# A second written order for a fused delta-rule attention and cosine feed-forward kernel

## The chip, the cores and the metric

The kernel runs on one core of a Trainium2 chip. The metric is device time in microseconds (us) of one execution. The core has five engines that run beside each other, each strictly in its own program order: TensorE (PE in the profile; its weight loads are PEld), VectorE (DVE), ScalarE (ACT), GpSimd (POOL) and SyncE (SP), which here only issues DMAs. Where one engine needs what another makes, it waits on a semaphore.

## The reference

There are two stages, in float32. The first is a gated delta rule, per batch and head, over 768 steps with a 48 x 48 state:

```python
k_n = k / (np.linalg.norm(k, axis=-1, keepdims=True) + 1e-06)
for t in range(S):
    y[:, :, t] = np.einsum('bhd,bhde->bhe', q[:, :, t], state)
    v_old = np.einsum('bhde,bhd->bhe', state, kt)
    state = state + bt[:, :, :, None] * np.einsum('bhd,bhe->bhde', kt, vt - v_old)
...
h = x @ w_in
g = h * np.cos(h)
return (g @ w_out).astype(np.float32)
```

Shapes: q, k, v are (4, 8, 768, 48), beta (4, 8, 768). The outputs of the 8 heads side by side are the 3072 x 384 input `x` of the second stage; `w_in` is 384 x 2048 and `w_out` 2048 x 384.

## The kernel before

**Attention.** The 768 steps are cut into 24 units of 32. For unit n, TensorE transposes keys and queries (`turn`, later units by DMA blocks and a VectorE transpose), multiplies them with each other (`gram`), and VectorE scales and masks the products (`gram_keys`, `gram_queries`). A unit needs the inverse of a unit triangular 32 x 32 matrix per head. For units 0 to 3 that is done by elimination on half blocks: `rows` (TensorE, L701) spreads rows, `eliminate` (L721, L728) subtracts them, on VectorE for units 0 and 1 (groups r = 0 and 1, four steps each) and on GpSimd for units 2 and 3 together (r = 2, eight steps, each fed by a copy on ScalarE, `rows_copy`). `fold`, `fold_in`, `fold_off` and `unfold` bring the blocks in and out. From unit 4 on, pairs m of units are inverted on GpSimd (`inv`, L791 and L798), with a round trip through DRAM before (`gram_put`, `gram_get`) and after (`put`, `get`). Then come `state` (products with the state), `right` (L843), `solve` (for the first units `solve_half`, `half_out`, `between`, `between_out` and `solve`), `solve_out` (L901), `update` and `update_out` (the new state), `within`, `within_out`, `features` and `features_out` (the transposed x). The step from one unit's state to the next is serial.

**Weights.** 28 pieces of the weights come in as 64-bit words and are made float32 by a chain per piece t: `weights` (DMA), `split` (ScalarE), `shift` (VectorE, two instructions, L497 and L502) and `add` (GpSimd, L506).

**Feed-forward.** Tokens go in 12 groups p of 256. For p = 0 and 1 the hidden layer is plain (`hidden`, L974), from p = 2 on it is a fast-multiplication scheme of 20 smaller products (`layer`, L1152) over sums of inputs (`x_sum`, L1067) and of weights (`in_sums`, L1114). The gate h cos h is four tasks: `turns` (ScalarE), `rest` (VectorE), `cos` (ScalarE), `gate` (VectorE, L1034). The output layer is plain for p = 0 (`out`, L1175) and a seven-product Strassen scheme after it (`out`, L1232), with sums `left` (L1248) and `right` with two indices (L1261), and results added up by `collect` (L1284).

**The order.** The program is a list of 2143 tasks, each with its emit function, its dependences and the buffers that it makes and uses. `Order.run` emits them in the order of `Order.LINE`, a written list of task numbers (the place of the task in the order in which it was added), and every engine's instructions are pinned in that order. No planner runs: an engine whose next task is not ready waits, with all that stands behind it. `Order.OTHER` is a set of tasks that run on their second engine: `fold` and `unfold` on ScalarE and not VectorE, `weigh`, `left`, `in_sums` and `right` on GpSimd and not VectorE, `x_sum` on VectorE and not GpSimd. Some buffers are scarce: the PSUM tag `h` has three banks, which `rows`, `hidden`, `layer` and the last group's products share; tag `two` has one, through which each of `turn`, `gram`, `solve` and `update` passes in turn.

## Time and profile before

| | |
|---|---|
| runs | 653.87, 645.26, 649.0 us, median 649.0 |
| the profiled execution | 647.59 us, its span 645.8 us |
| mean granted TensorE clock | 0.987 |
| busy | PE 616.5 us, PEld 577.8, DVE 509.5, POOL 450.7, ACT 266.4 |
| instructions | 28227, of which PE 12306 matmuls and as many weight loads |
| instruction queue q8 | 96 packets, 1.57 MB |

The page gives busy time and instructions of each engine, then the span in 40 slices of 16 us with the busy share in tenths and the granted clock of TensorE (PEclk), then the DMA queues, the chain that ended last, and groups of instructions with the idle time ahead of them and what ended it. The page's 40 slices average the clock; asked by its own edges, the trace grants half speed (0.50) from 32.03 to 38.86, from 45.69 to 52.51 and from 73.00 to 76.40 us, and full speed elsewhere as far as it records.

### The profile page before, as it was taken

How to read it: one execution, taken by the hardware profiler on the slowest of the kernel's cores; microseconds unless marked ns; L12 is line 12 of the kernel's file. 1: busy time of each engine (PE TensorE's matmuls, PEld its weight loads, DVE VectorE, ACT ScalarE, POOL GpSimd, SP SyncE). 2: the span in 40 equal slices, each digit the busy share in tenths (PEclk: the TensorE clock that was granted, in tenths of full speed). 3: DMA queues.
4: the chain of work that ended last, by engine and by line, in shares of the span. 5: the costliest groups of instructions: out<-in, count | busy, mean ns of one | idle time of the engine just before them, and what ended most of it. 6: DMA issues, size and time to landing. Idle time of an engine off the chain costs nothing.

```text
span 645.8 us, 28227 instructions
## 1 busy us (share of the span) xinstructions
PE 616.5 (95%) x12306; PEld 577.8 (89%) x12306; DVE 509.5 (79%) x948; ACT 266.4 (41%) x469; POOL 450.7 (70%) x788
## 2 busy tenths in 40 slices
PE   5869899999999999999999999999999999999997
PEld 4758788886989999999899999999999999999997
DVE  7788788889899988888788878766877668667681
ACT  3645556742233531631542533623533523435340
POOL 3347989888898888688789986797787584133103
PEclk9978899999999999999999999999999999999999
DMA  8882582664454554635424435513500403000001
GB/s 160 195 218 57 133 217 67 143 115 71 69 94 71 99 70 76 111 68 93 74 32 92 71 64 80 89 36 51 99 9 15 102 4 66 8 2 25 2 13 37
DMA packets 202923, 49.99 MB, mean 77 GB/s; under 512 B 194544, under 2 KB 197760, under 8 KB 202800
## 3 DMA queue, kind: packets, MB, share of 16 engines
q1 hardware_dynamic: 201536, 47.82, 38.6%
q8 instruction: 96, 1.57, 1.0%
q10 hardware_dynamic: 1088, 0.20, 0.2%
q0 software_dynamic: 176, 0.18, 0.1%
q14 instruction: 27, 0.22, 0.1%
HBM read 38.19 MB, written 9.96 MB: 75 GB/s over the span
## 4 chain that ended last, share of the span: by engine, by line
PE 75%; POOL 11%; DVE 7%; issue 3%; DMA 2%; SPq 1%; ACT 1%; POOLq 0%; DVEq 0%; ACTq 0%
PE p_out L1232 24%; PE p_h L1152 22%; PE p_h L974 7%; PE p_kq L828 4%; PE p_out L1175 3%; POOL z L798 3%; POOL part L791 3%; PE p_s L914 3%; PE p_u L891 2%; PE p_kq L931 2%; PE p_g L619 2%; PE p_o L1232 2%; DMA gb<-g_dr 1%; PE p_r L701 1%; POOL knrm L535 1%
## 5 line engine op out<-in xcount | busy, mean ns | idle before, releaser
L791 POOL TENSOR_TENSOR part<-z,gb 128x126 f32<-128x126 f32 (+22 forms) x310 | 139.8, 451 | 48.8 <-DMA gb<-g_dr 26.1
L798 POOL TENSOR_TENSOR z<-z,part 128x126 f32<-128x126 f32 (+22 forms) x310 | 139.4, 450 | 24.4 <-POOL part L791 0.2
L1232 PE MATMUL p_out<-w_out,g_ffn 128*128 128x192 f32 x672 | 121.2, 329 | 0.9 <-POOL part L791 0.4
L1232 PEld LDWEIGHTS p_out<-w_out,g_ffn 128*128 128x128 f32 x672 | 107.8, 190 | 2.4 <-POOL g_ffn L1248 0.7
L1031 ACT ACTIVATE turns<-turns,halfpi 128x512 f32<-128x512 f32 x96 | 68.9, 724 | 74.4 <-DVE turns L1022 73.8
L1232 PE MATMUL p_out<-w_sum,g_ffn 128*128 128x192 f32 x496 | 89.6, 329 | 1.6 <-DVE o L1284 1.6
L1248 POOL TENSOR_TENSOR g_ffn<-g_ffn 128x512 f32<-128x512 f32 x34 | 46.8, 1388 | 60.2 <-DVE g_ffn L1034 30.5
L1152 PE MATMUL p_h<-x_sum,w_in 128*128 128x128 f32 x640 | 84.4, 278 | 1.0 <-ACT g_ffn L1166 0.5
L1232 PEld LDWEIGHTS p_out<-w_sum,g_ffn 128*128 128x128 f32 x496 | 79.6, 190 | 2.5 <-DVE o L1284 1.8
L1152 PEld LDWEIGHTS p_h<-x_sum,w_in 128*128 128x128 f32 x640 | 78.3, 191 | 2.8 <-DVE g_ffn L1169 0.9
L1015 ACT ACTIVATE turns<-g_ffn,quarter_turn 128x512 int32<-128x512 f32 x70 | 50.1, 722 | 48.9 <-DVE g_ffn L1169 34.0
L1169 DVE TENSOR_TENSOR g_ffn<-g_ffn,p_h 128x512 f32<-128x512 f32 x80 | 54.3, 681 | 13.6 <-PE p_h L1152 12.0
L1034 DVE TENSOR_TENSOR g_ffn<-turns,g_ffn 128x512 f32<-128x512 f32 x70 | 54.7, 789 | 11.8 <-ACT turns L1031 11.7
L1022 DVE SCALAR_TENSOR_TENSOR turns<-g_ffn,turns 128x512 f32<-128x512 f32 x70 | 57.9, 834 | 5.7 <-ACT turns L1015 5.5
L1152 PE MATMUL p_h<-x_sum,in_sum 128*128 128x128 f32 x400 | 54.2, 279 | 0.3 <-issue 0.3
L1284 DVE SCALAR_TENSOR_TENSOR o<-p_out,o 128x192 f32<-128x192 f32 x74 | 25.2, 352 | 35.0 <-PE p_out L1232 31.2
L974 PE MATMUL p_h<-x_ffn,w_in 128*128 128x128 f32 x384 | 49.5, 290 | 1.6 <-ACT row_copies L712 1.6
L1152 PEld LDWEIGHTS p_h<-x_sum,in_sum 128*128 128x128 f32 x400 | 49.2, 191 | 1.3 <-issue 0.4
L974 PEld LDWEIGHTS p_h<-x_ffn,w_in 128*128 128x128 f32 x384 | 47.1, 203 | 2.5 <-ACT row_copies L712 1.7
L535 POOL TENSOR_TENSOR knrm<-ksum,halves 128x16 f32<-128x16 f32 (+1 forms) x14 | 37.5, 2678 | 15.9 <-DVE ksum L523 10.9
L1152 PE MATMUL p_h<-x_ffn,w_in 128*128 128x128 f32 x320 | 42.7, 277 | 0.0
L1248 DVE TENSOR_TENSOR g_ffn<-g_ffn 128x512 f32<-128x512 f32 x54 | 41.4, 769 | 0.5
(144 smaller groups left out, 1045.1 us busy)
## 6 DMA issues: line engine op xcount, KB each, us to landing
gb<-g_dr SPq DMA_DIRECT2D x20, 256.0 KB, 4.3
vp<-in_v_dram SPq DMA_DIRECT2D x96, 48.0 KB, 2.9
in_sum<-in_moe_w_out_dram SPq DMA_DIRECT2D x12, 384.0 KB, 4.6
out_dram<-o SPq DMA_DIRECT2D x23, 192.0 KB, 2.8
in_sum<-in_moe_w_in_dram SPq DMA_DIRECT2D x8, 512.0 KB, 4.3
kp<-in_k_dram SPq DMA_DIRECT2D x128, 24.0 KB, 2.2
z_dr<-z SPq DMA_DIRECT2D x10, 256.0 KB, 3.5
zt<-z_dr SPq DMA_DIRECT2D x80, 32.0 KB, 2.5
```

The source lines that it names most:

```text
L535: nc.gpsimd.tensor_tensor(out=scales[m][2][:, part], in0=sums[m, part.start][:, 0:n], in1=halves[:, 0:n], op=ALU.pow,)
L791: nc.gpsimd.tensor_tensor(out=part, in0=z[:, 0:rows, j, None].to_broadcast(shape), in1=a[:, j, None, j + 1 :].to_broadcast(shape), op=ALU. ...
L798: nc.gpsimd.tensor_tensor(out=behind, in0=behind, in1=part, op=ALU.subtract)
L974: nc.tensor.matmul(p_h[:, i], w_in[:, t, (4 * k + i) * 128 : (4 * k + i + 1) * 128], xts[p][:, t, unit * 128 : (unit + 1) * 128], start=(i ...
L1015: nc.scalar.activation(turns[p, f], hidden_of(p, f), AF.Identity, bias=quarter_turn, scale=TURN)
L1022: nc.vector.scalar_tensor_tensor(out=r, in0=hidden_of(p, f), scalar=TURN, in1=t, op0=ALU.mult, op1=ALU.subtract,)
L1031: nc.scalar.activation(r, r, AF.Sin, bias=halfpi, scale=2.0 * math.pi)
L1034: nc.vector.tensor_tensor(out=place(p, f), in0=step_of(rests.pop((p, f)), f), in1=step_of(hidden_of(p, f), f), op=ALU.mult,)
L1152: nc.tensor.matmul(p_h[:, e], in_block(*w)[:, e], x_of(p, b), start=new and e == 0, stop=True, skip_group_check=True,)
L1169: nc.vector.tensor_tensor(out=part_of(p, to), in0=part_of(p, one), in1=part_of(p, two), op=op)
L1232: nc.tensor.matmul(p_o, left(p, part, a)[:, e % 4], right(e, b), start=(e == 0), stop=(e == FT // 2 - 1), skip_group_check=True,)
L1248: either(("left", p, x, s), nc.vector, nc.gpsimd).tensor_tensor(out=left(p, s, to), in0=left(p, s, one), in1=left(p, s, two), op=op)
```

## The change

Only `Order.OTHER` and `Order.LINE` change. The 2143 tasks, their emit functions and dependences are the same, so TensorE has the same 12306 matmuls. What is said of the change was read from the lists by looking up each number's task.

Tasks that change engine:

- from ScalarE to VectorE: `fold` 0, `unfold` 0 and 1
- from GpSimd to VectorE: `in_sums` 6, 8, 14, 15
- from VectorE to GpSimd: `weigh` (1, 0), that is unit 2's values, and `right` (3, 6)
- `x_sum`: 25 tasks each way (65 of 110 stay the number on VectorE); `left`: 17 each way (34 of 88 stay the number on GpSimd)

The first tasks of TensorE, before and after (a task in brackets by unit, or group and step):

```
before: turn 0, turn 1, gram 0, gram 1, rows(0,0), rows(0,2), turn 2, rows(0,1), rows(1,2), rows(0,3), turn 3, rows(1,0), solve_half 0, between 0, solve 0, update 0, within 0, turn 4, rows(1,1), features 0, state 1, gram 2, rows(1,3), gram 3, hidden(0,0), rows(2,0), rows(2,1), rows(2,2), solve_half 1, between 1, hidden(0,2), solve 1
after:  turn 0, turn 1, gram 0, gram 1, rows(0,0), rows(0,1), rows(0,2), turn 2, rows(0,3), turn 3, rows(1,1), solve_half 0, rows(1,2), between 0, rows(1,0), solve 0, update 0, within 0, turn 4, state 1, features 0, gram 2, rows(1,3), gram 3, hidden(0,0), rows(2,0), rows(2,1), solve_half 1, rows(2,4), between 1, rows(2,2), solve 1
```

And of VectorE (sum, scale, spread belong to the norms of the keys; the second index is the unit of the pair):

```
before: picks 0, picks 1, sum(0,0), beta 0, sum(0,1), scale(0,0), scale(0,1), spread(0,0), spread(0,1), gram_keys 0, gram_queries 0, fold_in 0, gram_keys 1, gram_queries 1, begin_rows 0, fold_in 1, eliminate(0,0), eliminate(0,1), eliminate(0,2), eliminate(0,3), sum(1,0), shift 1, shift 0, shift 2, between_out 0, shift 3, sum(1,1), solve_out 0, shift 4, begin_rows 1, update_out 0, eliminate(1,0), scale(1,0), eliminate(1,1), gram_keys 2, gram_queries 2
after:  sum(0,0), sum(0,1), beta 0, picks 0, scale(0,1), scale(0,0), gram_keys 0, fold 0, fold_in 0, picks 1, gram_keys 1, begin_rows 0, gram_queries 1, gram_queries 0, fold_in 1, shift 0, eliminate(0,0), sum(1,0), eliminate(0,1), begin_rows 1, eliminate(0,2), eliminate(0,3), unfold 0, shift 1, scale(1,0), sum(1,1), shift 2, spread(0,0), between_out 0, shift 3, solve_out 0, scale(1,1), update_out 0, eliminate(1,0), sum(2,0), shift 4, eliminate(1,1), right 1, gram_keys 2, gram_queries 2
```

GpSimd's eight steps of `eliminate` for r = 2, with adds 7, 6 and 8 between them, stand in the same order in both. Further on, the tasks keep their places roughly: a task of TensorE moves by some tasks within its neighbourhood. SyncE's DMAs are permuted likewise. In the last group `left` (2, part 0) and `left` (1, part 1) run on GpSimd.

```diff
@@ class Order
     OTHER = {
-        ('weigh', 0, 0), ('fold', 0), ('unfold', 0), ('weigh', 0, 1), ('fold', 1), ('unfold', 1),
-        ('fold', 2), ('fold', 3), ('unfold', 2), ('unfold', 3), ('in_sums', 6), ('in_sums', 8),
-        ('in_sums', 14), ('in_sums', 15), ('x_sum', 2, 'd'), ('x_sum', 2, 'n'), ('x_sum', 2, 'm'),
...
+        ('weigh', 0, 0), ('weigh', 0, 1), ('fold', 1), ('weigh', 1, 0), ('fold', 2), ('fold', 3),
+        ('unfold', 2), ('unfold', 3), ('right', 3, 6), ('left', 1, 2, 1), ('left', 1, 4, 1),
...
     LINE = """
-2031 0 1 9 10 2 3 15 16 17 11 54 55 18 56 57 21 4 60 22 23 19 58 61 62 6 24 25 26 27 28 30 34 63 64
-29 93 92 101 65 66 32 102 31 2032 2035 2036 73 95 33 35 36 37 14 123 39 20 40 96 97 2037 2039 2038
...
+2031 0 92 1 2 3 15 4 16 17 21 54 55 56 11 9 2035 6 57 7 22 18 93 14 60 123 61 23 24 2039 26 5 27 62
+28 2032 10 63 30 29 65 64 95 32 25 66 2033 34 31 96 39 101 2043 2036 126 67 33 68 35 102 36 124 2047
...
```

## The prediction, made before the changed kernel was run

> **What bounds the kernel now.** I read busy time by engine and the slices first, then TensorE's waits on both sides of 100 us.

> ```profile
> PE 616.5 (95%) x12306; PEld 577.8 (89%) x12306; DVE 509.5 (79%) x948; ACT 266.4 (41%) x469; POOL 450.7 (70%) x788
> PE   5869899999999999999999999999999999999997
> DVE  7788788889899988888788878766877668667681
> POOL 3347989888898888688789986797787584133103
> ```

> TensorE is the bound, busy 616.5 of 645.8 us, and most of what it lacks lies in the first five slices (80 us). From 100 us on its table of waits is nearly empty:

> ```profile
> PE p_out L1232 <- DVE o L1284: 1.7, 2, 1.6
> PE p_u L891 <- DMA zt<-z_dr: 1.5, 1, 1.5
> PE p_h L1152 <- ACT g_ffn L1166: 0.5, 1, 0.5
> ```

> These and five shorter ones (0.4, 0.4, 0.3, 0.3, 0.2) make 5.3 us in 546. The order changes no work of TensorE, so there it can win 5 us and lose more. Up to 100 us the table has 6.4 us for the first loads, which both orders share, and some 13 us of other waits.

> The opening is a serial chain through VectorE: eliminate unit 0, solve it, update the state, eliminate unit 1, `gram 3`, and the first hidden layer at 49.03 us. The timeline of VectorE shows where the order costs time in it:

> ```profile
> 20.50 0.24 DVE L721 TENSOR_TENSOR rows<-rows,p_r 128x88 f32<-128x88 f32 x1 [2.57 <-PE p_r L701]
> ...
> 28.73 1.49 DVE L497 SCALAR_TENSOR_TENSOR in_sum<-in_sum 128x512 uint32<-128x512 uint32 x1 [0.53 <-ACT in_sum L493]
> 30.13 1.51 DVE L502 TENSOR_SCALAR w_in<-w_in 128x512 uint32<-128x512 uint32 x1
> 31.57 0.54 DVE L876 TENSOR_TENSOR u_half<-vp,p_v 128x384 f32<-128x384 f32 x1
> ...
> 40.47 1.33 DVE L728 TENSOR_TENSOR rows<-rows 128x96 f32<-128x96 f32 x1
> ```

> VectorE waits 2.57 us for `rows(0,1)`, which stands behind `rows(0,2)` and `turn 2` on TensorE. `shift 2` takes 1.49 + 1.51, where others of its kind take 0.68 + 0.41, with `between_out 0` (L876) queued behind it. An instruction of `eliminate` takes 1.33 instead of 0.27. Both slow stretches lie beside adds of GpSimd (28.38 to 31.36, and 40.39 to 41.67), so I take those as the cause.

> The arrival of instructions shows on TensorE's timeline and in the queue table:

> ```profile
> 45.99 0.44 PE L619 MATMUL p_g<-kq_t 48*32 48x64 f32 x10 [1.88 <-DVE knrm L546]
> 48.01 1.09 PE L619 MATMUL p_g<-kq_t 48*32 48x64 f32 x54 [1.58 <-issue]
> 92.21 0.79 PE L931 MATMUL p_kq<-u,tt 32*32 32x48 f32 x52 [0.91 <-issue]
> q8 instruction: 96, 1.57, 1.0%
> ```

> "issue" is a wait for nothing that the profile shows. It falls inside `gram 3` and `within 2`. Numbering TensorE's instructions (weight loads, matmuls, semaphore waits) from the start, the breaks lie at places 705, 1473, 2497 and 3521, whole multiples of 256 apart; q8's 96 packets of 16 KB are about as many as such blocks. So arrival is a real cost, but all issue waits in the two tables of TensorE sum to 3.7 us (1.6, 0.9, 0.4 and 0.3, 0.2 before 100 us, 0.3 behind).

> **The change, part by part**, against the profiled execution, 647.6 us (span 645.8 and 1.8 around it); the median shown, 649.0, is 1.4 above it. Under 2%, 13 us, a measurement of this kernel tells little: its own runs spread over 1.3%.

> (1) *Unit 0's elimination.* `rows(0,1)` follows `rows(0,0)`; two such tasks take 3.62 from 13.48, so it ends at 17.1, before step 0 is through. The 2.57 goes. But ahead of step 0 VectorE now has `picks 1` (1.08), `shift 0` (1.09) and `fold 0` (not shown on VectorE; 0.22 by the 128x128 copy L691, bounds 0.17 by the 128x8 product L551 and 0.41 by the 128x512 shift L502), partly in its waits of 0.14 and 0.96: start 16.7 for 15.54. Steps 0 to 3 take 2.39, 2.13, 1.87 and 1.23, with `sum(1,0)` and `begin_rows 1` between (0.47, 0.15): end 25.0 for 25.86. **-0.9.** Late next is `unfold 0`, on VectorE 2 x 0.22 where ScalarE took 0.79: 25.4 for 26.6. `solve_half 0` starts when `rows(1,1)` is off TensorE, 25.7 for 27.64. **-1.9** so far.

> (2) *Its solve.* `rows(1,2)` (some 1.5 at this clock) now lies in the hole ahead of `between 0`, 0.65 long, and overfills it: 28.5 for 29.61. `between_out 0` needs VectorE past `shift 1`, `scale(1,0)`, `sum(1,1)`, `shift 2` and a spread: 1.03 + 0.8 + 0.5 + 1.03 + 0.1 = 3.5 from 25.4, thus 28.9; if adds block `shift 2` as before, 1.9 later. `between 0` itself ends at 29.4. Bounds 0.8 and 2.2 earlier than 31.57; I take **-1.7** in all, nearer the unblocked row. From `solve 0` to `update_out 0` what leaves VectorE (`sum(1,1)`, `begin_rows 1`, `shift 4`) and what enters (`scale(1,1)`) lies in its waits of 0.71 and 0.75: nothing, and at worst +0.8.

> (3) *Unit 1's elimination.* From 37.94 to the end of `gram_queries 2` (45.84) are 7.9 us. Adds 1 to 3 are through by then, so `eliminate(1,0)` should take 2.4 for 3.85; `scale(1,0)` (1.3 there) has moved up; `sum(2,0)` 0.86, `shift 4` 1.02 and `right 1` 0.47 come in. 7.45, or 8.9 if it is blocked as now. **-0.45**, bound +1.0. `gram 3` waits for `gram_queries 2` alone, so the first hidden layer starts **2.2** earlier, bounds 0 and, if the issue wait went with it, 4. The same 23 tasks stand ahead of `gram 3`, so its block edge stays where it is, and I leave the 1.58.

> (4) *50 to 100 us.* The chain is GpSimd's eight steps for units 2 and 3, 55.23 to 77.7, fed by `rows(2,0)` behind the hidden layer. Their order, adds among them, is the same, so the 2.2 is carried. `rows(2,4)` has moved ahead of `rows(2,2)` and holds one of three banks until step 2; `rows(2,3)` then needs `gate(0,0)` for a bank. Cost 0, as step 3 starts only at 68.6; at worst one bank's wait as at 73.22, 1.55. Here 1.0 of the 1.7 issue waits behind 50 us goes if the count is right.

> (5) *100 to 215 us.* VectorE is nearly full: 90.7 us busy of 100 to 200 by tens of us. The four `in_sums` (18 on VectorE average 0.9), `fold` and `unfold` add 4.8; `weigh` (0.96) and `right(3,6)` (0.7) leave; by place in the order, 3 to 4 us more VectorE work stands ahead of `layer` and `solve` of units 6 and 7 than now. VectorE starts 2.2 earlier and has 9.3 us of idle to use. I charge **+0.6**. The extra work is hidden by that idle time; without it, +4.

> (6) *The rest.* From 240 on VectorE is 62 to 83% busy by fifties, and GpSimd has 4 us less in all and 10 less ahead of unit 16. The last group's POOL sums `left` end before their products as now (0.2 to 1.2 us of slack by the rows at 628 to 638). Of 5.3 us of waits I let 0.5 go. DMAs: SyncE has the same 616 tasks' DMAs; `put 2` now stands behind `weights 26`, `weights 27` and three loads of blocks, whose own conditions come before `inv`'s end. Nothing, unless a release is late.

> Sum: -2.2 - 1.0 + 0.6 - 0.5 = -3.1: **644.5 us**.

> [...] The issue waits above are 3.7 us by row. [...]

> **The rivals.** (A) *Forecast*: opening 0 to 4 earlier, the rest as summed, 641 to 647. Chance 0.5. (B) *The opening gains far more*: half clock is granted for 17 us (32.03 to 38.86, 45.69 to 52.51, 73.00 to 76.40), and hidden tasks there take 4.59 and 4.45 where 2.94 is usual. If fuller work keeps the clock up, 1.6 + 1.5, with 4 for the chain, all 3.7 of arrival and half of the 5.3: 13.5, so 634. For: `rows(1,2)` fills a hole. Against: `gram 3` still waits, and it was such waits that stood ahead of both windows. 0.15. (C) *Arrival cannot be ordered away*: every order has the same 96 edges, and a run `state`, `gram` is 384 instructions in some 2 us. The 1.0 stays, or up to three new breaks of 0.9 come (`gram 11`, `state 20`, behind `state 21`, where by my count two edges lie under 2.5 us apart): 645.5 to 648. 0.15. [...] (D) *Slower, by VectorE at 130 to 215 us*: its in-order queue makes products of p = 1 and layers of p = 2 wait for `right`, `x_sum` and `solve_out`. It decides if less than 2 of those 9.3 us can be used, since 4 more stand ahead and 2.2 come from the opening. Price up to 4, plus the opening's gain returned: 648 to 652. For: it is 94 and 96% busy in the two tens from 180 to 200. Against: idle time before TensorE's results shrinks with it. 0.13. (E) *A late release behind the order's back*, such as `inv` of units 8 and 9: it ends at 218.2 and `solve 8` starts at 227.2, with `put` and `get` taking nearly all between; 1.3 us more GpSimd work stands ahead, and each of several pairs could lose 2: 655 to 663. 0.07.

> **How the numbers follow.** The likeliest case gives 644.5. From 636 to 654 holds A, C, D and the near half of B and E: about 0.85; I widen the lower end to 635. Faster by over 2% (under 636): most of B, 0.12. Slower by over 2%: the far end of E and what I don't see, 0.08.

> **What would show it.** Right: no wait of 2.57 at the second step of `eliminate`; `shift 2` near 1.1; first hidden task at 46 to 47.5; GpSimd's eight steps ending at 75 to 76; waits from 100 us on still under 8 us. Wrong: `shift 2` or `eliminate(1,0)` slowed again, so that `gram 3` starts at 46 as now; VectorE at the head of TensorE's waits between 130 and 215 us; issue waits of 4 us or more.

## The result, and the profile after

| | before | after |
|---|---|---|
| median | 649.52 us (645.26 to 653.87) | 667.26 us (666.56 to 667.87) |
| ratio, 95% interval | | 1.0273 [1.0203, 1.0342] |
| profiled execution, its span | 647.59, 645.8 us | 667.87, 665.8 us |
| waits of TensorE from 100 us on | 5.3 us | 15.7 us |
| half clock from 100 us to the last product | none | 20.5 us |

The changed kernel is 2.7% slower; forecast were 644.5 us, a gain too small to tell from none. The page of the changed kernel, busy time of TensorE and VectorE with its 40 slices and the granted clock in tenths:

```profile
PE 626.4 (94%) x12306; PEld 586.4 (88%) x12306; DVE 500.2 (75%) x955; ACT 262.5 (39%) x464; POOL 440.0 (66%) x786
...
PE   5878899999999999999999799999988999999998
...
DVE  6988889799778877878878667867767458557671
...
PEclk9999999999979999989999799999999899999999
```

TensorE's row has dips behind the opening that it did not have before (the 7 in slice 23, the 8s in 30 and 31), and the clock falls to 7 or 8 tenths in slices 12, 18, 23 and 32. (The nines of the first 40 us don't mean full speed: the trace's records of the clock begin at 40.68 us, at 28.62 us before, and ahead of them eight products of `rows` take 1.81 us that take 1.00 at full clock.) The same 12306 matmuls are busy for 9.9 us longer: they ran slower. The table of TensorE's waits from 100 us on (total us, times, longest):

```profile
PE p_u L890 <- DMA zt<-z_dr: 4.8, 6, 2.6
PE p_kq L827 <- DVE st L921: 3.1, 1, 3.1
PE p_h L1151 <- ACT g_ffn L1165: 2.9, 1, 2.9
PE p_out L1231 <- DVE g_ffn L1247: 2.3, 2, 1.5
PE p_h L1151 <- ACT p_h L1163: 1.6, 2, 1.2
...
PE p_w L857 <- issue: 0.3, 1, 0.3
```

Three shorter rows are left out (0.3, 0.2, 0.2): 15.7 us in all, 10.4 more than before. The stretches of half clock, cut out by their own edges (start:end, length, busy time by engine; the figure in front of the last two is the granted clock):

```profile
184.03:190.85 6.82, 6.35 (x96) 5.88 (x100) 2.74 (x7) 0.00 (x0) 5.40 (x16) 0.50 0.38 77
289.84:293.25 3.41, 3.41 (x12) 3.41 (x13) 2.82 (x5) 0.00 (x0) 2.99 (x6) 0.50 0.63 83
375.18:382.00 6.82, 5.66 (x121) 5.42 (x108) 6.45 (x13) 2.98 (x5) 6.04 (x11) 0.50 0.60 80
518.53:521.95 3.42, 3.42 (x15) 3.42 (x15) 0.30 (x1) 1.58 (x3) 0.67 (x3) 0.50 0.75 140
```

TensorE is busy for 18.8 us in them (second figure); by estimate that is work of 9.4 us at full clock, so 9.4 are lost. **The account:** waits +10.4, half clock +9.4, together 19.8 of the 20.0 us by which the span grew. Up to 100 us the two orders come out about even (20.3 and 19.8 us of waits there; at half speed for 45.7 and 44.1 us by estimate, counting the stretch ahead of the records, where those `rows` took 1.81 us for 1.00, as half speed).

Each stretch of half clock begins behind a wait. TensorE's timeline at the first (start, length, matmuls, and in brackets the idle time ahead):

```profile
180.86 1.05 PE L1151 MATMUL p_h<-x_sum,in_sum 128*128 128x128 f32 x8
184.50 2.14 PE L890 MATMUL p_u<-rhs,zt 32*32 32x48 f32 x64 [2.58 <-DMA zt<-z_dr]
186.57 3.78 PE L1151 MATMUL p_h<-x_sum,w_in 128*128 128x128 f32 x16
```

TensorE waits 2.58 us for the inverse of unit 6; then two layer tasks take 1.89 us each where one took 1.05.

**What the five places wait for**, followed back task by task:

| us | TensorE's task | its wait | what stands ahead, on which engine | half clock |
|---|---|---|---|---|
| 182 | `solve 6` | 2.58 | GpSimd: `inv` of units 6 and 7 ends at 178.2 for 173.7 before; it begins 1.5 later and takes 37.4 for 34.5 | 6.82 |
| 287 | `solve 11` | 1.5 in 3 pieces | SyncE: its `get` stands behind 21 loads and stores | 3.41 |
| 371 | `state 15` | 3.14 | SyncE, then VectorE: `update_out 14` behind `turn_out 18`, which waits for blocks | 6.82 |
| 495 | `out`(7,2,1) | 1.5 | GpSimd: `left`(7,1,1) behind step 3 of `inv` (4.7 us) | none |
| 514 | `layer`(9,1) | 2.9 | GpSimd: `left`(7,3,0), whose end frees a gate tile, behind step 6 of `inv` (6.7 us) | 3.42 |

Only the fourth has an engine that the change assigned anew (`left`(7,1,1) was on VectorE). For the second and third, SyncE's timeline (start, length, DMAs):

```profile
261.09 0.55 SPq L801 DMA_DIRECT2D z_dr<-z  x1
...
267.99 2.02 SPq L810 DMA_DIRECT2D zt<-z_dr  x4
270.04 3.36 SPq L350 DMA_DIRECT2D vp<-in_v_dram  x4
273.44 2.04 SPq L361 DMA_DIRECT2D qp<-in_q_dram  x4
275.53 1.53 SPq L1295 DMA_DIRECT2D out_dram<-o  x1
277.11 2.24 SPq L361 DMA_DIRECT2D qp<-in_k_dram  x4
279.45 4.72 SPq L350 DMA_DIRECT2D kp<-in_k_dram  x8
284.27 3.18 SPq L810 DMA_DIRECT2D zt<-z_dr  x4
...
355.42 0.36 SPq L801 DMA_DIRECT2D z_dr<-z  x1
...
362.80 3.30 SPq L361 DMA_DIRECT2D qp<-in_k_dram  x4
366.15 2.09 SPq L361 DMA_DIRECT2D qp<-in_q_dram  x4
```

The store of the inverse of units 10 and 11 is issued at 261.1; unit 10's part is fetched at 268, unit 11's only at 284, behind 14 us of issuing. At 355.4 SyncE issues the store of the inverse of units 14 and 15, for which it had stood 7.0 us with the blocks of unit 18 queued behind; these blocks land so late that VectorE, in its own timeline,

```profile
371.92 1.25 DVE L603 STREAM_TRANSPOSE kq_t<-qp 128x1024 f32<-128x1024 f32 x1 [5.10 <-DMA kp<-in_k_dram]
373.09 0.92 DVE L921 TENSOR_TENSOR st<-st,p_s 128x768 f32<-128x768 f32 x1
```

waits 5.10 us ahead of `turn_out 18` (the transpose) and makes the state (L921) afterwards, though `update 14` had ended at 367.4. The slack from the end of issuing `get` to `solve` tells the same: units 6, 7 and 11 had 4.3, 7.2 and 11.1 us before, now 0.9, 0.8 and 0.1.

### The profile page after: what moved, and what is told of

It is laid out like the page before. It is cut to its first block, busy times and chain, and to the rows that moved or that the text cites. A ratio compares the mean times of both kernels' runs of the same rounds, so it can differ in the third digit from the quotient of the medians.

```text
span 665.8 us, 28220 instructions
## 1 busy us (share of the span) xinstructions
PE 626.4 (94%) x12306; PEld 586.4 (88%) x12306; DVE 500.2 (75%) x955; ACT 262.5 (39%) x464; POOL 440.0 (66%) x786
## 3 DMA queue, kind: packets, MB, share of 16 engines
q8 instruction: 96, 1.57, 1.0%
## 4 chain that ended last, share of the span: by engine, by line
PE 55%; POOL 17%; SPq 8%; DMA 7%; DVE 7%; issue 4%; ACT 2%; POOLq 0%; DVEq 0%; ACTq 0%
PE p_out L1231 20%; PE p_h L1151 18%; POOL z L797 7%; POOL part L790 7%; PE p_h L973 5%; SPq L350 4%; PE p_kq L827 2%; PE p_s L913 2%; PE p_u L890 2%; PE p_kq L930 2%; PE p_o L1231 2%; POOL g_ffn L1247 2%; DMA gb<-g_dr 1%; DMA in_sum<-in_moe_w_in_dram 1%; DMA zt<-z_dr 1%
## 5 line engine op out<-in xcount | busy, mean ns | idle before, releaser
L790 POOL TENSOR_TENSOR part<-z,gb 128x126 f32<-128x126 f32 (+22 forms) x310 | 135.3, 437 | 56.6 <-DMA gb<-g_dr 30.2
L797 POOL TENSOR_TENSOR z<-z,part 128x126 f32<-128x126 f32 (+22 forms) x310 | 144.1, 465 | 24.3
L1231 PE MATMUL p_out<-w_out,g_ffn 128*128 128x192 f32 x672 | 124.6, 334 | 0.2 <-DVE o L1283 0.2
L1231 PEld LDWEIGHTS p_out<-w_out,g_ffn 128*128 128x128 f32 x672 | 110.0, 193 | 1.6 <-issue 0.4
L1247 POOL TENSOR_TENSOR g_ffn<-g_ffn 128x512 f32<-128x512 f32 x34 | 44.3, 1311 | 70.5 <-PE p_out L1231 24.1
L1151 PEld LDWEIGHTS p_h<-x_sum,w_in 128*128 128x128 f32 x640 | 80.3, 197 | 4.5 <-POOL x_sum L1066 3.2
L1168 DVE TENSOR_TENSOR g_ffn<-g_ffn,p_h 128x512 f32<-128x512 f32 x80 | 54.2, 681 | 21.1 <-PE p_h L1151 19.8
L1021 DVE SCALAR_TENSOR_TENSOR turns<-g_ffn,turns 128x512 f32<-128x512 f32 x70 | 54.8, 788 | 16.1 <-ACT turns L1014 15.9
L1033 DVE TENSOR_TENSOR g_ffn<-turns,g_ffn 128x512 f32<-128x512 f32 x70 | 52.8, 762 | 3.1 <-ACT turns L1030 3.1
L1151 PEld LDWEIGHTS p_h<-x_sum,in_sum 128*128 128x128 f32 x400 | 50.9, 197 | 2.7 <-ACT p_h L1163 1.4
L973 PE MATMUL p_h<-x_ffn,w_in 128*128 128x128 f32 x384 | 47.5, 282 | 1.7 <-issue 1.2
L973 PEld LDWEIGHTS p_h<-x_ffn,w_in 128*128 128x128 f32 x384 | 45.0, 195 | 2.7 <-issue 1.4
```

The costliest lines, as they stand in the source:

```text
L790: nc.gpsimd.tensor_tensor(out=part, in0=z[:, 0:rows, j, None].to_broadcast(shape), in1=a[:, j, None, j + 1 :].to_broadcast(shape), op=ALU. ...
L797: nc.gpsimd.tensor_tensor(out=behind, in0=behind, in1=part, op=ALU.subtract)
L973: nc.tensor.matmul(p_h[:, i], w_in[:, t, (4 * k + i) * 128 : (4 * k + i + 1) * 128], xts[p][:, t, unit * 128 : (unit + 1) * 128], start=(i ...
L1021: nc.vector.scalar_tensor_tensor(out=r, in0=hidden_of(p, f), scalar=TURN, in1=t, op0=ALU.mult, op1=ALU.subtract,)
L1033: nc.vector.tensor_tensor(out=place(p, f), in0=step_of(rests.pop((p, f)), f), in1=step_of(hidden_of(p, f), f), op=ALU.mult,)
L1151: nc.tensor.matmul(p_h[:, e], in_block(*w)[:, e], x_of(p, b), start=new and e == 0, stop=True, skip_group_check=True,)
```

## The experiments

**Order and engines apart.** Each part of the change alone. The first kernel has the set `OTHER` of before in the changed kernel, the second the new set in the kernel before:

```diff
 class Order:
-    OTHER = {...new...}
+    OTHER = {...as before...}
     LINE = """...new..."""
```

> The new order, with every sum on the engine where the kernel before has it. Theory Q (the new order puts tasks that something waits for behind long or waiting tasks in the in-order queues of SyncE, GpSimd and VectorE; TensorE's waits at 181, 286, 371, 495 and 514 us and the half clock behind them are the loss): only the wait at 495 us, for a POOL sum behind a step of the inverse, comes from a changed engine, so 663 to 668 us. Theory E (the sums that changed engine are the loss): back to 647 to 652 us. Theory I (instructions arrive later in the new order): nothing changes, 666 to 668 us.

> The order of the kernel before, with every sum on the engine where the changed kernel has it. Theory Q: the order is what loses, so 647 to 655 us. Theory E: 660 us or more. Theory I: as before, 648 to 650 us.

Measured: **686.42 us**, ratio 1.0594 [1.0526, 1.0662], and **721.32 us**, 1.1103 [1.1044, 1.1163]. The first misses every expectation; the second meets only theory E's "660 us or more", and E is refuted by the first. The new order with the old engines is 19 us slower than with its own, the old order with the new engines 73 us slower. Half clock behind 100 us is 23.9 and 61.4 us. An order and a choice of engines belong together here; neither part of the change can be blamed alone.

**One engine's sequence exchanged.** SyncE's tasks of the kernel before in the new sequence; and GpSimd's tasks of the changed kernel in the old one. In effect (the kernels have the merged lists of numbers written out):

```diff
-LINE = before
+LINE = before, with its SyncE tasks in the sequence of after, each as early as its dependences and buffers allow
```

> The kernel before, with SyncE's tasks (loads, stores, the passages of gram and inverse through memory) in the changed kernel's sequence; the sequence on the four other engines is that of before. Theory Qs (SyncE's queue is the main cause: it stands still at 140 to 160 and 240 to 260 us behind a store that waits, and is full behind, 56 of 60 us from 180 to 240): most of the loss comes with it, 657 to 668 us. Theory Qa (no single queue: the loss comes from several of them): 650 to 657 us. Theory M (a mixture of two sequences that were each found as a whole is slower than both): 670 us or more.

> The changed kernel, with GpSimd's tasks behind its first 48 in the sequence of the kernel before; 96 of them stand elsewhere than in the changed kernel, the sequence on the other engines and all engines are those of the changed kernel. Theory Qp (GpSimd's sequence, with sums behind steps of the inverse, is the main cause): 648 to 656 us. Theory Qs: 664 to 669 us, since SyncE's waits at 178, 261 and 348 us stay. Theory M: 675 us or more.

Measured: **715.51 us**, 1.0996 [1.0932, 1.1061], and **728.59 us**, 1.1193 [1.1118, 1.1268]: theory M in both. So neither of these two queues can be called the cause by exchange; in these two kernels a sequence was bad beside four that it was not written with. The three other queues were not exchanged.

**Cut in time.** The two orders have done nearly the same tasks at any place, so one can take over from the other, with its engines:

```diff
-line = old
+line = new[:440] + [t for t in old if t not in new[:440]]
```

> Order and engines of the changed kernel for its first 440 tasks (to about 139 us), those of the kernel before for all others. Theory Q (the loss is in separate places behind 178 us, each a task behind a long or waiting one in an in-order queue): the new opening costs nothing, so 646 to 650 us, as the excess of TensorE's tasks up to 140 us is 36.7 us before and 36.0 after. Rival S (the opening leaves SyncE, GpSimd and VectorE in a state from which the later order must lose): 655 us or more.

> Order and engines of the kernel before for the first 440 tasks, those of the changed kernel for all others. Theory Q: 665 to 670 us. Rival S: 655 us or less.

> Order and engines of the changed kernel for its first 1000 tasks (to 304 us of its own time), those of the kernel before for the rest; at this place the two orders have done the same tasks but for four each. Theory Q (the loss is local: each stretch of the new order loses what its trace shows there, whatever follows): up to 300 us the excess of TensorE's tasks is 54.9 us in the changed kernel and 46.3 before, 8.6 more; with 648.3 for the kernel before, 657 us, range 654 to 660. Theory C (what is lost in one stretch is caught up or paid again in the next): 651 us or less, or 664 and more.

> The reverse: the kernel before for the first 1000 tasks, the changed kernel for the rest. Theory Q: the changed kernel's excess behind 300 us is 26.5 us for 15.4 before, 11.1 more: 659 us, range 656 to 663. Theory C: 651 us or less, or 666 and more.

Measured: new_to_139 **649.55 us**, 1.0001 [0.9969, 1.0033]; old_to_139 **677.49**, 1.0420 [1.0357, 1.0483]; new_to_300 **671.67**, 1.0304 [1.0266, 1.0343]; old_to_300 **661.62**, 1.0142 [1.0102, 1.0183].

As measured, new_to_139 meets theory Q, and old_to_300 does (659, range 656 to 663); old_to_139 misses both theories, and new_to_300 lies in theory C's range of 664 and more. The new opening is worth nothing, and the old one doesn't help the new order. For what follows I use the excess: the time from one TensorE task to the next, less the usual time of its kind. Two of the four have a loss at the seam, where one order finds the other's queues otherwise filled: 12.3 us of excess of the tasks that begin from 120 to 140 us in old_to_139 (0.8 and 0.7 in the kernels themselves), 11.5 of them one wait of `update` for VectorE that ends at 153.1 us, and 18.2 from 300 to 360 in new_to_300 (5.8 before), most of it one wait of 13 us for `solve 12`. Without those 11.6 and 12.4 us they would be at 666 and 659 us; theory Q gave 665 to 670 and 657. old_to_300, without such a loss, is 10.3 us above its kernel before; the trace had 11.1. So where the seam costs nothing, a stretch loses about what its own trace shows; for the two others that holds only after the seam's loss is taken off, which the theory had not allowed for.

**Places put right.** All these kernels have one more loop in `Order.run`, and differ in the list of moves (each: the tasks, and the task behind which they go):

```diff
         line = [keys[int(i)] for i in self.LINE.split()]
+        for moved, behind in self.MOVES:
+            line = [t for t in line if t not in moved]
+            at = line.index(behind) + 1
+            line[at:at] = moved
```

```diff
+    MOVES = (    # blocks18_first
+        ([('blocks', 18, 0), ('blocks', 18, 1)], ('gram_put', 17)),
+    MOVES = (    # norms4_early
+        ([('norms', 4, 0)], ('inv', 2, 6)),
+    MOVES = (    # six_moved
+        ([('layer_out', 2, 18), ('collect', 1, 6), ('layer', 2, 0), ('out', 1, 3, 0)], ('layer', 2, 11)),
+        ([('get', 7)], ('blocks', 10, 0)),
+        ([('get', 11)], ('get', 10)),
+        ([('blocks', 18, 0), ('blocks', 18, 1)], ('gram_put', 17)),
+        ([('inv', 10, 3)], ('left', 7, 1, 1)),
+        ([('inv', 10, 6), ('put', 10), ('gram_get', 11)], ('x_sum', 9, 'g')),
```

> The changed kernel with one of these six moves alone: the two block loads of unit 18 are issued by SyncE ahead of the store of unit 7's inverse, for which SyncE now stands waiting 7 us. Theory Q: the wait of 3.1 us at 371 us goes, and with it those of 1.7 and 1.2 behind it and the half clock from 375 to 382 us: 6.8 us less, 660.5 us (range 659 to 664). Without the clock's part, 3 to 4 us less, about 663.5 us. Theories E and I: no change, 666 to 668 us.

Measured: **664.38 us** (661.71 to 669.16), 1.0238 [1.0173, 1.0304]; the profiled span is 660.0 us for 665.8. In the trace the wait at 371 us and the half clock behind it are gone: the excess from 360 to 380 us is 1.8 us for 7.1. The place was what the trace said. ("The store of unit 7's inverse" in the expectations is that of pair 7, units 14 and 15.) But the median won only 2.9 us, within the spread of its own runs and outside theory Q's 659 to 664, and the shorter span is not the move's alone: half clock behind 100 us is 6.8 us in this trace for 20.5, since the stretches at 289 and 518 us are missing too, the latter behind a wait of 3.1 us of the same task.

> The changed kernel with one task moved: GpSimd makes norms(4,0) (3.2 us) right behind step 6 of the inverse of units 4 and 5, at 127.2 us, where it stands idle until 130.1 us, instead of ahead of step 0 of the inverse of units 6 and 7. Theory Q: that inverse begins 2.8 us earlier (137.9 us, when its tile is ready), its loads reach the solve of unit 6 before TensorE does, and the excess of 6.0 us at 181 to 190 us (a wait of 2.75 and half clock behind it) goes: 661 us, range 659 to 665. Theory M (what is put right in one place makes another late): 665 us or more.

Measured: **665.98 us**, 1.0264 [1.0201, 1.0327]. The inverse began at 140.3 us and not 137.9: with `norms` away, GpSimd waited 1.6 us for the next thing in line, the load of the gram. TensorE's timeline in this kernel:

```profile
183.54 1.59 PE L897 MATMUL p_u<-rhs,zt 32*32 32x48 f32 x64 [1.07 <-DMA zt<-z_dr]
...
201.67 2.74 PE L897 MATMUL p_u<-rhs,zt 32*32 32x48 f32 x64 [3.42 <-DMA zt<-z_dr]
204.34 2.08 PE L1158 MATMUL p_h<-x_ffn,w_in 128*128 128x128 f32 x8
```

The wait ahead of `solve 6` fell from 2.58 to 1.07, with no half clock behind it, and all of it came back 18 us later: `solve 7` begins at 201.67 us, to the hundredth where it began in the changed kernel, because its loads stand on SyncE behind five groups of others. Now TensorE waits 3.42 us for it, and half clock follows (200.5 to 207.3).

> The changed kernel with six groups of tasks put elsewhere in its order, all engines and all other places as they are: two tasks of TensorE ahead of the solve of unit 6; the loads of the inverse for units 7 and 11 ahead of loads that nobody waits for yet; the two block loads of unit 18 ahead of the wait for the inverse of unit 14; one POOL sum ahead of a step of the inverse, and two of another group ahead of another. Theory Q: the excess of the tasks at these places over their usual time sums to 6.0 (181 us), 1.0 (202), 3.8 (286), 6.8 (370), 1.7 (494) and 4.2 (513), together 23.5 us of the 667.3, waits and half clock; if nothing else is late behind them, 644 us; with some of it lost to the next wait, up to 653 us. Theory I: the number of TensorE instructions and their blocks are the same, so 662 us or more. Theory E: 660 us or more, since the engines stay.

> The changed kernel with five places put right: layer(2,0) and out(1,3,0) ahead of the solve of unit 6 on TensorE; the loads of the inverse for unit 11 right behind those for unit 10, and the block loads of unit 18 ahead of the store of unit 7's inverse, on SyncE; step 3 of the inverse of units 20 and 21 behind the sum left(7,1,1) on GpSimd; left(7,3,0) off GpSimd and two sums of weights of group 9 on VectorE instead of GpSimd. Theory Q, by what the excess at these places was in the changed kernel and where it was put right in the two runs that tried it: 2.8 (181 us), 2.7 (286), 5.3 (370), 1.0 (494) and 4.2 (513), 16.0 us: 651 us, range 648 to 657 with a new wait or two. Theory I (arrival of instructions): 662 us or more. Theory M (each place that is put right makes another late): 660 us or more.

The diffs of repaired and repaired2, beside moves of six_moved:

```diff
     # repaired: without the moves of get 7 and of inv(10,6); instead of the latter
+    OTHER -= {('left', 7, 3, 0)}
+    OTHER |= {('x_sum', 9, 'g'), ('x_sum', 9, 'h')}
     # repaired2: as repaired, without the move of layer(2,0) and out(1,3,0), and with
+        ([('norms', 4, 0)], ('inv', 2, 6)),
+        ([('get', 7)], ('blocks', 10, 0)),
+        ([('store', 1, 0)], ('blocks', 12, 1)),
+        ([('eye', 11), ('inv', 11, 0), ('inv', 11, 1)], ('layer_out', 9, 9)),
```

> The changed kernel with all places put right whose cause the traces name: norms(4,0) as in the run norms4_early; the loads of the inverse for unit 7 ahead of the loads v(8), blocks(11,1) and v(9), and the store of group 1 ahead of the store of unit 8's gram, on SyncE; unit 11's loads, unit 18's block loads, step 3 of the inverse of units 20 and 21 as in the run repaired; left(7,3,0) and two sums of weights on VectorE instead of GpSimd; the unit matrix for units 22 and 23 (ScalarE, it has to wait until the inverse of units 20 and 21 has left the one tile) behind four outputs of layers instead of ahead of them. Theory Q: 6.0 (181 us), 1.0 (202), 2.7 (286), 5.3 (370), 1.0 (494), 4.2 (513): 20 us less, 647 us, range 646 to 656 with a new wait or two. Theory M: 660 us or more.

Measured: six_moved **665.13 us**, 1.0244 [1.0196, 1.0292]; repaired **665.02**, 1.0264 [1.0226, 1.0302]; repaired2 **664.06**, 1.0227 [1.0153, 1.0301]. Of the 16 to 23 us that the places had cost, 0.6 to 3 came back by the ratios: theory M in the two for which it was stated. (The number of six_moved alone would also fit theories E and I; engines_back stands against E, the changed kernel's own issue waits against I.) Most places moved are quiet in the traces (370 us in all three, 287 and 495), and others stand up, one of 1.3 to 1.7 us at 501 to 503 us in all three. ScalarE's waits say how, in six_moved and in repaired:

```profile
ACT o L1282 <- DMA out_dram<-o: 4.2, 1, 4.2
```

```profile
ACT z L787 <- DMA z_dr<-z: 9.1, 1, 9.1
```

In six_moved the loads of unit 7, put forward on SyncE, push a store back; ScalarE waits 4.2 us for the tile that it empties, and TensorE 2.6 us for ScalarE (at 227 us). In repaired the unit matrix for units 22 and 23 waits 9.1 us on ScalarE until the one tile of the inverse is empty, with the outputs of four layers queued behind; TensorE waits 6.6 us. In six_moved the same task of ScalarE waits 8.7 us, and TensorE 6.1. Before the repair that had been hidden behind the late sum on GpSimd. repaired2 moves both out of the way, and TensorE waits 3.2 us at 228 and 3.6 us at 519 us, until the loads of other inverses land, those of units 8 and 20.

> The kernel before with its own two late releases behind 100 us put right: on VectorE the copy-out collect(1,6) ahead of in_sums(12) (TensorE's wait of 1.6 us at 181 us), on SyncE the store of the inverse of units 12 and 13 ahead of the store of unit 15's gram, and the loads of it right behind (the wait of 1.5 us at 308 us). If a late release costs its wait and nothing follows: 645.3 us, 3.1 less. If it is paid again elsewhere, as in norms4_early: 647 to 650 us; if the order is so tight that a move makes something else late: 652 us or more.

```diff
+    MOVES = (    # in the kernel before
+        ([('in_sums', 12)], ('collect', 1, 6)),
+        ([('gram_put', 15), ('get', 12)], ('put', 6)),
```

Measured: **652.63 us**, 1.0027 [0.9997, 1.0057]. The two moves didn't help the kernel before: its wait at 181 us shrank from 1.6 to 0.4, the one at 308 stayed (1.7 us in two pieces for 1.5), and a new one of 3.5 us, for `solve 13`, came at 325 us. The next inverse on GpSimd began at 316.3 us for 309.5, and with it the norms behind its second step came later, and VectorE's `right`, for which the solve waits. By the ratio the gain was paid again elsewhere; the median would fit the third expectation, but its comparison median is 651.33 us. No kernel that was run beats the one before clear of the noise.

**The arrival of instructions.**

> The kernel before with 64 matmuls of 16x16 (64 weight loads and 64 matmuls) ahead of TensorE's first work, where it waits for the first loads; their result is not used. They shift every later instruction of TensorE by half a block of 256. Theory I (what a wait costs hangs on where the blocks' edges fall, so that an order found for one place of the edges is worse with another): the issue waits, 3.7 us before, come at other tasks and sum to 8 us or more, 655 us or more. Theory Q (arrival is a small cost wherever the edges fall): issue waits of 2 to 6 us, 647 to 653 us.

```diff
+    for _ in range(64):
+        nc.tensor.matmul(bank("kq", [16, 16], "p_shift"), tiny.rearrange("p a h -> p (a h)"),
+            halves.rearrange("p a h -> p (a h)"), start=True, stop=True)
```

Measured: **661.69 us**, 1.0199 [1.0158, 1.0239], and neither this number nor the trace answers the question. The 64 calls became 128 products (x128 in the trace) and 128 weight loads, 256 instructions: one whole block (in the kernel before the breaks lie whole multiples of 256 apart) and not half of one, so the edges stay at the same tasks. The wait inside `gram 3` is there again, 1.5 us for 1.58, 257 places later among TensorE's instructions. And the products took 18.7 us (5.57 to 24.27), where TensorE's first work had begun at 4.45, so the whole kernel started late. That arrival is a small part of the loss is read from the changed kernel itself, whose order puts other tasks at the edges: its issue waits are 3.1 us in all, for 3.7 before. What half a block would do was not tested.

**A wait of known length.** Behind `out`(10,1,1) of the kernel before, at 600 us:

```diff
+    def hold():
+        p = bank("kq", [128, 48], "p_hold")
+        nc.tensor.matmul(p, ident, ident[:, 0:48], start=True, stop=True)
+        chain = [p] + [work.tile([128, 48], FP, name="chain", bufs=2) for _ in range(4)]
+        for a, b in zip(chain, chain[1:]):
+            nc.scalar.copy(b, a)
+        p = bank("kq", [128, 48], "p_hold")
+        nc.tensor.matmul(p, ident, chain[-1], start=True, stop=True)
```

> The kernel before with one wait put into it at 600 us, where the other engines have time: behind out(10,1,1) TensorE makes a small product, ScalarE copies it 4 times from tile to tile, and TensorE goes on with a product of the last copy. A wait of some 1.3 us. Theory C (a wait of TensorE of more than some 2 us is followed by half clock, a shorter one isn't, as the waits behind 100 us in the traces so far show it): no half clock behind it. Theory N (the stretches of half clock have another cause): none either.

> The same with 10 copies, a wait of some 2.8 us. Theory C: half clock for 3.4 us or 6.8 us, beginning 2 to 5 us behind the start of the wait, and the tasks in it take twice their time: 1.7 to 3.4 us more than the wait. Theory N: no half clock there, and the tasks behind the wait take their usual 0.89 (layer) and 1.30 us (out).

The diff is that of hold_4; the others have 10 and 16 copies. hold_4 and hold_10 took 649.66 and 651.02 us in one run each, beside 648.31 us. TensorE waits 1.07 us at 600 us in the one, 2.65 in the other, and no half clock follows: the clock's theory C falls in that form. hold_16, also one run, 655.93 us beside 648.17, waits 4.23 us, and it follows. TensorE's timelines of hold_10 and of hold_16:

```profile
602.98 0.42 PE L1779 MATMUL p_hold<-chain,consts 128*128 128x48 f32 x2 [2.65 <-ACT chain L1777]
603.23 1.12 PE L1154 MATMUL p_h<-x_ffn,in_sum 128*128 128x128 f32 x8
604.19 1.06 PE L1154 MATMUL p_h<-x_sum,w_in 128*128 128x128 f32 x8
```

```profile
605.65 0.66 PE L1779 MATMUL p_hold<-chain,consts 128*128 128x48 f32 x2 [4.23 <-ACT chain L1777]
606.11 2.04 PE L1154 MATMUL p_h<-x_ffn,in_sum 128*128 128x128 f32 x8
607.95 1.92 PE L1154 MATMUL p_h<-x_sum,w_in 128*128 128x128 f32 x8
```

The same two tasks take 1.12 and 1.06 us in the one and 2.04 and 1.92 in the other. In each trace all changes of the clock lie whole multiples of 3.41 us apart. Cut along that grid, hold_10's wait falls into two pieces; hold_16's takes two thirds of one (columns as above):

```profile
598.57:601.98 3.41, 1.75 (x13) 1.63 (x11) 0.95 (x2) 1.43 (x7) 0.36 (x1) 1.00 0.00 0
601.98:605.40 3.42, 2.42 (x20) 2.43 (x21) 0.80 (x2) 2.57 (x7) 0.00 (x0) 1.00 0.02 5
```

```profile
600.28:603.69 3.41, 1.14 (x9) 1.02 (x7) 0.95 (x2) 1.98 (x9) 0.00 (x0) 1.00 0.00 0
603.69:607.11 3.42, 1.46 (x7) 1.46 (x8) 0.40 (x1) 2.76 (x10) 0.00 (x0) 0.50 0.00 0
```

Pieces that are 51 and 71% busy (1.75 and 2.42 of 3.41) leave the clock up; one of 33% is followed by half clock. All 20 traces of this case, cut in that way from 60 us to the last product, show what follows a piece at full clock:

| TensorE busy in the piece | next piece at full clock | at half clock |
|---|---|---|
| under 0.4 | 0 | 45 |
| 0.4 to 0.7 | 71 | 27 |
| over 0.7 | 3247 | 0 |

Theory W holds, also in the six traces alone that were taken after it was stated (8 of 8 pieces under 0.4, none of 981 over 0.7). Between 0.4 and 0.7 both happen, and what decides there stays open.

## Why the prediction was wrong

**(1) Unit 0's elimination.** The 2.57 us wait went, as said, and step 1 follows step 0 without a gap. But what was to end at 25.0 us ended at 26.96. VectorE's timeline of the changed kernel:

```profile
21.85 0.78 DVE L727 TENSOR_TENSOR rows<-rows 128x64 f32<-128x64 f32 x1
22.55 1.32 DVE L690 COPY rows<-eye 128x128 f32<-128x128 f32 x1
...
29.52 1.26 DVE L496 SCALAR_TENSOR_TENSOR in_sum<-in_sum 128x512 uint32<-128x512 uint32 x1
30.70 1.51 DVE L501 TENSOR_SCALAR w_in<-w_in 128x512 uint32<-128x512 uint32 x1
32.13 0.17 DVE L557 TENSOR_TENSOR bz<-bs,consts 128x16 f32<-128x16 f32 x1
32.80 0.56 DVE L875 TENSOR_TENSOR u_half<-vp,p_v 128x384 f32<-128x384 f32 x1 [0.50 <-issue]
```

Step 0 began at 17.20, not 16.7; step 1 took 2.67 for 2.13; and `begin_rows 1` (L690), counted at 0.15, took 1.32. `solve_half 0` started at 27.90, not 25.7: `unfold 0` ended at 27.49, and TensorE had waited 1.89 us inside `turn 3` for the queries of unit 3 and so left `rows(1,1)` only at 27.97. I had not looked up where that load lands. **(2)** `shift 2` was slowed just as before (1.26 + 1.51), and `solve 0` began at 34.56 for 32.16: +2.4 where -1.7 was forecast. Part of this is the late start. Another part is TensorE's clock, which I had at full speed here as before. The product of `between 0` before, then the same one in the changed kernel, `rows(1,0)` and `solve 0`:

```profile
29.61 0.88 PE L858 MATMUL p_v<-u_half,halves_z 32*32 32x48 f32 x64 [0.65 <-ACT u_half L868]
```

```profile
31.18 1.50 PE L857 MATMUL p_v<-u_half,halves_z 32*32 32x48 f32 x64
32.61 2.02 PE L700 MATMUL p_r<-rows,w_sum 128*128 128x120 f32 x8
34.56 1.50 PE L890 MATMUL p_u<-u_half,halves_z 32*32 32x48 f32 x64
```

`between 0` takes 1.50 for 0.88: it lies ahead of the first record of full clock, which is at 40.68 us and not at 28.62. And `rows(1,0)` now stands ahead of `solve 0`, which I had not charged: it holds TensorE 1.2 us beyond the end of `between_out 0` (33.36). **(3)** held by itself: from the end of `update_out 0` (39.93) to that of `gram_queries 2` (47.56) are 7.6 us, 7.45 forecast. `gram 3` began 1.7 us later than before, and yet the first hidden task came at 48.89 for 49.03, because the issue wait of 1.58 inside `gram 3` was gone, the gain that I had left out. So the opening's -2.2 came to -0.1, and even that by luck: without the vanished issue wait it would have been a loss. **(4)** came near: GpSimd's eight steps ended 1.5 earlier where 2.2 were to be carried, at 76.21 for 77.74, and `out`(0,0,0) began 0.9 earlier. The arrival itself: issue waits are 3.1 us for 3.7, between the forecast (1.0 less) and rival C (none less); two of them, 1.2 and 1.0 us, stand at new places. Issue waits are small in both kernels (3.7 and 3.1 us in all at some 96 edges, by the 96 packets of q8 in each): there was little to win. Rival B had the clock gain from fuller work. It did not, though its windows of half clock shrank from 17.1 to 3.4 us: the stretch ahead of the first record of full clock grew by 12.1 us instead.

**(5) and (6)** are where the prediction failed. The stretch from 130 to 215 us was named, with the wrong engine: VectorE heads none of TensorE's waits there; what came late was GpSimd's inverse of units 6 and 7 (+4.4 us) and SyncE behind it. And for the rest I let 0.5 us go with the sentence "Nothing, unless a release is late". Five releases were. The mechanism is rival E's, at other units than the one it names (units 8 and 9 lose nothing), with a chance of 0.07 that was far too low and a price of 655 to 663 us that was too small by the clock: I charged waits of 2 us and not the half clock behind them, 9.4 of the 20 us. I had the slack of some pairs from the old trace, but never went through the new order queue by queue to see what now stands ahead of each `get`, `update_out` and `left`; 21 loads and stores ahead of unit 11's `get` could be read in the list.

**What is shown and what is not.** Shown: in the traces the loss is waits and half clock at those places (the account; old_to_300 finds that of the later part again); a move at one place takes its wait away or shortens it; and no set of moves gave more than 3 us back, in norms4_early since the next release in the same chain was late as well. Argued, not shown: that each of the five late releases by itself costs what stands in its row, since no run got that time back. Open: how much of the loss would remain for an order with the new opening in which all five queues are arranged anew; whether GpSimd's inverse of units 6 and 7 takes 3.0 us longer because VectorE is busier beside it. For the latter speaks that its first three steps took 4.14, 4.54 and 4.99 us for 3.10, 3.71 and 4.31, while VectorE was busy 14.11 of 15 us for 8.90 of 12; no run took that apart.

## What to carry to other kernels

Where every queue is written out by hand, read a new order queue by queue, and ask for each task that another engine needs what now stands ahead of it in its own queue and for what that one waits; the slack of a release in the old trace is the price at which it begins to count. Charge a wait of TensorE that fills most of one piece of the clock's grid about twice (an estimate from this case: 10.4 us more of waits came with 9.4 us lost at half clock). And allow for a stall that is taken away at one place of a chain through several in-order queues to come back at the next one, as it did here: measure the whole, not the place.

## What the runs had that was not expected

- **How busy TensorE was in one piece of 3.41 us at full clock told the clock of the next**: half clock behind 45 of 45 pieces under 0.4, behind none of 3247 over 0.7. TensorE 2.65 us idle across an edge of the grid cost nothing more (hold_10); 2.58 us in the changed kernel, most of it within one piece (0.38 busy), was followed by 6.82 us at half clock. One and the same task waits 2.9 us in the changed kernel, with 3.42 us of half clock behind it, and 3.1 us in blocks18_first, where an edge at 510.1 us cuts the wait (pieces 0.60 and 0.50 busy), with none. The edges lie elsewhere from trace to trace (one at 28.62 us before, one at 40.68 in the changed kernel, 3.5 pieces later), so by estimate the same wait can be cheap in one execution and dear in the next.
- **Order and engines are one thing.** Two lists that take 649.5 and 667.3 us with their own engines take 721 and 686 with each other's, and 716 and 729 with one queue's sequence exchanged (SyncE's and GpSimd's).
- **A single buffer carries a delay across engines**: the one tile of the inverse held ScalarE for 9.1 us, and with it the outputs of layers that have nothing to do with it.
